# Attention and two expert layers in one Trainium2 kernel: the routing of the last batch issued in groups, and the weight pieces of the first slots split by one engine

## The chip, the core and the metric

The kernel runs on one core of a Trainium2 chip. The core has a matrix engine (TensorE, PE in the rows, with its weight loads as PEld), a vector engine (VectorE, DVE), a scalar engine (ScalarE, ACT), a general engine (GpSimd, POOL) and a sync engine (SyncE, SP) that here only issues transfers. Each engine works through its own list of instructions in the order in which the kernel was written, and waits at an instruction until what it needs is there. The metric is the device time of one execution in microseconds; lower is better.

## The reference, cut to what matters

```python
# attention, 4 batches x 12 heads x 448 rows x 64, scores capped with tanh
scores = cap * np.tanh(scale * np.matmul(q, k.T) / cap)
...
# a dense layer, 1792 rows x 768, hidden width 1536
(silu(x @ w_gate) * (x @ w_val)) @ w_out
# a routed layer, 8 experts, 768 -> 1024 -> 768
do_compute = x @ w_skip > 0
e_idx = np.argmax(x @ w_route, axis=1)
gate_w = softmax(x @ w_route)[arange, e_idx]
for e in range(8):
    h = np.maximum(x[e_idx == e] @ w1[e], 0.0)
    y[e_idx == e] = gate_w * (h @ w2[e])
out[do_compute] = x + y
```

## The kernel before, in words

**Batches.** Attention and the dense layer run batch by batch. The dense layer of a batch is 36 *units* of 18 matmuls each, so 144 units in all (`W_END`); a unit w multiplies with weights that ACT rounds (`wh`) and DVE turns into a remainder (`wl`), because every product is made of three: high times high, high times low, low times high.

**Slots.** The routed layer works in *slots*: 128 rows that go to one expert. Slot 0 and the expert of slot 1 (`FETCHED = 2`) are chosen while batch 3 is still in the dense layer, from batches 0 to 2 alone. The rest (which rows go to slots 1 to 7, and the experts of slots 2 to 7) is known only when the last batch has been routed. A slot takes eight *pieces* of expert weights, 128 x 1536 numbers each. Four go into `first(0)` to `first(3)`, nine matmuls each into `ph`, then a relu into `hid` and a transpose through `tp` into `rh` and `rl` (high and low part of the hidden rows); four go into `second(0)` to `second(3)`, twelve matmuls each into `py`. `finish` multiplies with the gate, adds the rows (`o`) and scatters them to the output.

**A piece's way.** SP loads it into a raw buffer (`load_next`), ACT copies its high part (`gh`, line 915), an engine subtracts for the low part (`gl`, line 356), PE uses both, and the pair of buffers serves again. `split_next` does the two steps in the middle. From slot 1 on (`so["auto"]`) each call of `piece()` first splits ahead until as many pieces are ready as there are pairs.

**Between the dense layer and slot 1.** What each engine does from unit 144 on is written out by hand in the table `LATE`: `first` and `second` are PE's work for slot 0, `splitV` and `splitP` split a piece on DVE or on POOL, and each `route` is one step of `last_routed`, the routing of the last batch. That is a chain of some 40 small DVE instructions: `choose` (which expert), a product on PE (`count_up`, into `last`), `ranks`, `last_tiles`, `places`, `last_at`, `entries`, a second product on PE (`listed`, line 257), which gives the row numbers (`idx`) for the gathers, then `experts` (`es`, which SP waits for before it can load slot 2) and at the end `gates`, whose list needs a third product. `turn_h` makes `rh` on ACT and `rl` on DVE; `turn_x(1)` transposes the gathered rows of slot 1.

**Rooms.** Before, 14 raw buffers and 4 pairs; a pair is taken in a fixed rotation.

Of the kernel before, what the change touches and what calls it, by code (L numbers as in the profile page):

```python
# [26 lines left out]

LENGTHS = (5, 6, 5, 6, 5, 5)

NOW = 7  # L30


STEPS = {0: 6, 1: 2, 2: 3, 3: 3, 4: 3, 5: 4, None: 4}
# [24 lines left out]
    chain store  # L58
""".split()
LATE = """  # L60
    route route route route route route route route route route splitV first1 route route route route route
    route route route splitP route route route route route hidden0 first2 route route route splitP route route
    route route first3 route splitV hidden1 second0 route route route splitP route splitP route second1 second2
    route route route route route route route route route route route splitV route rows1 gather gather second3
    route route splitV gather gather gather gather
""".split()


# [1 line left out]
def tile_attn_moe_moe(  # L70
# [311 lines left out]
    def whole(exact):  # L382
        with ExitStack() as ph:
# [449 lines left out]
            def open_early():  # L833
                right.close()
                _, pool = pools("right")
                p = pool("early", 1)
                psum = pool("ps_e", 1, space=PSUM)
                so["raw"] += [x[:, 0:PIECE] for x in pair_room + [head_room]]
                so["raw"] += [p.tile([128, PIECE], F32, name="raw3")]
                so["pair"] += [[p.tile([128, PIECE], F32R, name=f"{n}{i}") for n in ("gh", "gl")] for i in range(3)]  # L840
                so["xg"].append(p.tile([128, DM], F32, name="xg0"))
                so["x"] = [p.tile([128, KD, 128], F32R, name=n) for n in ("xgh", "xgl")]
                so["h"] = [[p.tile([128, KF2 // 2, 128], F32R, name=f"{n}{i}") for n in ("rh", "rl")] for i in range(2)]
                so["room"] = p.tile([128, 1024], F32, name="big_room")[0:T]
                so["row"] = p.tile([128, S], F32, name="row2")
                so["ph"] = [psum.tile([128, 512], F32, name=f"ph{i}") for i in range(2)]
                so["tp"] = [psum.tile([128, 512], F32, name=f"tp{i}") for i in range(2)]
                nc.gpsimd.memset(so["xg"][0], 0.0)

            def open_late():  # L850
                left.close()
                _, pool = pools("left")
                p = pool("late", 1)
                psum = pool("ps_l", 1, space=PSUM)
                so["xg"] += [p.tile([128, DM], F32, name=f"xg{i}") for i in range(1, NSTATIC)]
                raws_ = [p.tile([128, PIECE], F32, name=f"raw{i}") for i in range(7, 14)]
                so["raw"] += raws_[:NOW]
                so["spare"] = raws_[NOW:]
                so["pair"] += [[p.tile([128, PIECE], F32R, name=f"{n}3") for n in ("gh", "gl")]]
                so["late"] = p.tile([T, 1600], F32, name="late_room")  # L860
                so["hid"] = p.tile([128, F2], F32, name="hid")
                so["o"] = [p.tile([128, DM], F32, name=f"o{i}") for i in range(3)]
                so["last"] = psum.tile([128, 512], F32, name="last")
                so["py"] = psum.tile([128, 2, 512], F32, name="py")
                for xg in so["xg"][1:]:
                    nc.gpsimd.memset(xg, 0.0)
# [9 lines left out]
                    bounds_check=end - 1, oob_is_err=False,  # L876
                )

            def turned(high, low, src):
# [7 lines left out]
                split_low(nc.vector, low, tp, high)  # L887
# [6 lines left out]
            def turn_h(half):  # L894
                rh, rl = so["h"][half]
                turned(rh, rl, so["hid"][:, 512 * half:512 * half + 512])


            coming, todo, held, ready, made = [], [], [], [], [0]

            def load_next():
                while so["raw"] and not todo:
# [6 lines left out]
                load_piece(held[-1], todo.pop(0))  # L909
                return True  # L910

            def split_next(engine):
                raw = held.pop(0)
                wh, wl = so["pair"][made[0] % len(so["pair"])]
                nc.scalar.copy(wh, raw)  # L915
                split_low(engine, wl, raw, wh)
                so["raw"].append(raw)
                made[0] += 1
                ready.append((wh, wl))

            def begin_loads():
                coming.extend(range(FETCHED))
# [3 lines left out]
            def piece():  # L926
                while load_next():
                    pass
                while so["auto"] and held and len(ready) < len(so["pair"]):
                    split_next(nc.vector)  # L930
                return ready.pop(0)

            def mm3_(ps, sh, sl, wh, wl, start, stop):
# [4 lines left out]
            def first(i):  # L938

                xh, xl = so["x"]  # L940
                half, k0 = i // 2, 3 * (i % 2)
                wh, wl = piece()
                for kk in range(3):
                    c = slice(512 * kk, 512 * kk + 512)
                    mm3_(so["ph"][half], xh[:, k0 + kk], xl[:, k0 + kk], wh[:, c], wl[:, c],
                         k0 + kk == 0, k0 + kk == KD - 1)
                if i % 2:
                    nc.scalar.activation(
                        out=so["hid"][:, 512 * half:512 * half + 512], in_=so["ph"][half], func=ACTF.Relu
                    )  # L950

            def second(i):

                rh, rl = so["h"][i // 2]
                wh, wl = piece()
                HD = DM // 2
                for f in range(2):
                    f2 = 2 * (i % 2) + f
                    for half in range(2):
                        c = slice(DM * f + HD * half, DM * f + HD * half + HD)  # L960
                        mm3_(so["py"][:, half, 0:HD], rh[:, f2], rl[:, f2], wh[:, c], wl[:, c],
                             i == 0 and f == 0, i == 3 and f == 1)

            def finish(s):
                HD = DM // 2
# [185 lines left out]
            for w in range(W_END):  # L1151
# [22 lines left out]
            open_late()  # L1174


            def last_routed():
                b = B - 1
                last, take = so["last"], scratch(so["late"])
                yield from choose(b, take)  # L1180
                yield count_up(b, last)
                yield from ranks(b, take)
                yield from last_tiles(take)
                yield from places(b, take)
                yield from last_at(b, take)
                rt.pop("ah", None)
                yield from entries(b, rt["at"], (tok,), take)
                yield listed(last[:, 0:MAXSLOT])
                V.tensor_tensor(idx, lists[:, 0], last[:, 0:MAXSLOT], op=ALU.add)
                yield next_gathered()  # L1190
                so["raw"] += so["spare"]
                while load_next():
                    pass
                yield from experts(take)
                coming.extend(range(FETCHED, NSTATIC))
                yield from gates(b)
                yield from entries(b, rt["at"], (gate,), take)
                yield listed(last[:, 64:64 + MAXSLOT])
                yield V.tensor_tensor(lists[:, 1], lists[:, 1], last[:, 64:64 + MAXSLOT], op=ALU.add)

            gathered = iter(range(1, NSTATIC))

            def next_gathered():
# [1 line left out]
                    gather(s)  # L1205
                    return

            routing = last_routed()
            so["auto"] = False
            late = {  # L1210
                "route": lambda: next(routing, None), "splitV": lambda: split_next(V),
                "splitP": lambda: split_next(nc.gpsimd), "first1": lambda: first(1), "first2": lambda: first(2),
                "first3": lambda: first(3), "hidden0": lambda: turn_h(0), "hidden1": lambda: turn_h(1),
                "second0": lambda: second(0), "second1": lambda: second(1), "second2": lambda: second(2),
                "second3": lambda: second(3), "rows1": lambda: turn_x(1), "gather": next_gathered,
            }
            for name in LATE:
                late[name]()
            any(False for _ in routing)
            any(gather(s) for s in gathered)  # L1220
            so["auto"] = True
            finish(0)
# [104 lines left out]
```

## Time and profile before

| | us |
|---|---|
| median of 3 runs | 933.44 |
| lowest and highest | 932.9, 936.52 |
| the profiled execution, device time | 933.06 |
| its span in the profile | 930.8 |
| PE busy | 897.0 (96%) |
| DVE busy | 635.2 (68%) |
| ACT busy | 509.0 (55%) |
| POOL busy | 124.3 (13%) |

The span is the time from the first to the last instruction of the profiled execution; 2.3 us of its device time lie around it. The shares are averages over stages of different kinds.

### The profile page before, as it was taken

The numbers are of one execution on the slowest core, as the hardware profiler recorded it, in microseconds if no ns is written. First come the engines' busy times: TensorE is split into PE (matmuls) and PEld (weight loads), VectorE is DVE, ScalarE is ACT, GpSimd is POOL, SyncE is SP. The second block draws the span as 40 slices with busy tenths as digits, with TensorE's granted clock in tenths as the row PEclk, the third lists the DMA queues.
The fourth block names the chain that finished last, engine by engine and source line by source line (L and its number), as shares of the span: only waits on it lengthen the run. The fifth ranks groups of instructions, "written<-read, shape, count | busy, mean of one in ns | idle before, by whom it ended". The sixth has DMA issues, their size and how long they took to land.

```text
span 930.8 us, 12697 instructions
## 1 busy us (share of the span) xinstructions
PE 897.0 (96%) x4708; PEld 700.5 (75%) x4708; DVE 635.2 (68%) x916; ACT 509.0 (55%) x587; POOL 124.3 (13%) x76
## 2 busy tenths in 40 slices
PE   5999999999899999999999999999999995999996
PEld 2336776677567877777777877889999885988996
DVE  1868999897736755736566664446755458899994
ACT  5996675666355455545554546233333432778883
POOL 1000000000002221122302223000000036311001
PEclk9999999999899999999999999999999997899999
DMA  6996888888668234432744222453364373999940
GB/s 125 212 239 180 232 247 245 234 230 242 155 128 199 79 93 128 98 93 62 180 120 127 88 93 68 97 129 137 118 226 165 81 217 126 378 392 397 395 178 7
DMA packets 226336, 161.50 MB, mean 174 GB/s; under 512 B 159180, under 2 KB 186828, under 8 KB 226256
## 3 DMA queue, kind: packets, MB, share of 16 engines
q1 hardware_dynamic: 224048, 157.12, 58.8%
q0 software_dynamic: 1280, 3.16, 0.9%
q8 instruction: 41, 0.67, 0.3%
q14 instruction: 39, 0.32, 0.1%
q10 hardware_dynamic: 928, 0.23, 0.1%
HBM read 140.80 MB, written 22.81 MB: 176 GB/s over the span
## 4 chain that ended last, share of the span: by engine, by line
PE 89%; DVE 3%; ACT 3%; SPq 2%; issue 1%; DMA 1%; POOL 0%; POOLq 0%; DVEq 0%
PE mo L681 20%; PE mo L682 19%; PE mo L683 19%; PE ps L459 7%; PE bank L514 6%; PE py L936 2%; PE py L934 2%; PE py L935 2%; PE ph L934 2%; PE ph L935 2%; PE ph L936 2%; PE mo L548 1%; SPq L370 1%; PE tp L885 1%; PE mo L751 1%
## 5 line engine op out<-in xcount | busy, mean ns | idle before, releaser
L681 PE MATMUL mo<-xhl,wh 128*128 128x448 f32 x576 | 215.0, 373 | 0.0
L683 PE MATMUL mo<-xhl,wl 128*128 128x448 f32 x576 | 210.4, 365 | 0.0
L682 PE MATMUL mo<-xhl,wh 128*128 128x448 f32 x576 | 210.3, 365 | 0.0
L356 DVE TENSOR_TENSOR wl<-raw,wh 128x768 fp32r<-128x768 f32 x108 | 115.3, 1068 | 76.4 <-ACT wh L668 75.0
L668 ACT CAST wh<-raw 128x768 fp32r<-128x768 f32 x108 | 89.7, 831 | 87.5 <-PE mo L682 62.6
L681 PEld LDWEIGHTS mo<-xhl,wh 128*128 128x128 f32 x576 | 108.1, 188 | 27.3 <-issue 8.1
L683 PEld LDWEIGHTS mo<-xhl,wl 128*128 128x128 f32 x576 | 108.2, 188 | 8.9 <-DVE wl L356 0.2
L682 PEld LDWEIGHTS mo<-xhl,wh 128*128 128x128 f32 x576 | 108.3, 188 | 7.9
L681 PE MATMUL mo<-hh,wh 128*128 128x448 f32 x288 | 108.4, 376 | 1.0 <-ACT x L728 1.0
L682 PE MATMUL mo<-hl,wh 128*128 128x448 f32 x288 | 105.5, 366 | 0.0
L683 PE MATMUL mo<-hh,wl 128*128 128x448 f32 x288 | 105.4, 366 | 0.0
L720 ACT ACTIVATE s<-mo 128x448 f32<-128x448 f32 x48 | 26.0, 541 | 114.3 <-PE mo L683 111.4
L459 PE MATMUL ps<-qkt 64*112 64x448 f32 x368 | 82.6, 568 | 0.0
L503 POOL TENSOR_TENSOR sums<-arena 112x896 f32<-112x896 f32 x11 | 23.2, 2113 | 393.4 <-ACT arena L475 393.4
L468 ACT ACTIVATE arena<-ps,inv_sb 112x896 f32<-112x896 f32 x72 | 68.7, 1006 | 5.4 <-PE ps L459 5.3
L475 ACT ACTIVATE arena<-arena,cap_sb 112x1792 f32<-112x1792 f32 x36 | 64.5, 1793 | 1.1
L681 PEld LDWEIGHTS mo<-hh,wh 128*128 128x128 f32 x288 | 54.3, 188 | 14.0 <-issue 7.9
L356 DVE TENSOR_TENSOR gl<-raw,gh 128x1536 fp32r<-128x1536 f32 x33 | 57.7, 1757 | 6.4 <-ACT gh L915 5.8
L723 DVE SCALAR_TENSOR_TENSOR s<-s,mo 128x448 f32<-128x448 f32 x48 | 29.6, 617 | 42.8 <-PE mo L683 42.5
L683 PEld LDWEIGHTS mo<-hh,wl 128*128 128x128 f32 x288 | 54.2, 188 | 4.6
L682 PEld LDWEIGHTS mo<-hl,wh 128*128 128x128 f32 x288 | 54.3, 188 | 4.0
L514 PE MATMUL bank<-arena,arena 112*64 112x448 f32 x264 | 54.9, 548 | 1.7 <-ACT arena L475 0.8
(241 smaller groups left out, 1434.3 us busy)
## 6 DMA issues: line engine op xcount, KB each, us to landing
raw<-ws SPq DMA_DIRECT2D x54, 768.0 KB, 4.6
raw<-in_moe_w_dram SPq DMA_DIRECT2D x33, 768.0 KB, 12.5
ws<-w SPq DMA_DIRECT2D x36, 384.0 KB, 5.8
more<-in_moe_w_dram SPq DMA_DIRECT2D x15, 768.0 KB, 13.2
raw<-in_moe_w_gate_dram SPq DMA_DIRECT2D x12, 768.0 KB, 5.6
raw<-in_moe_w_val_dram SPq DMA_DIRECT2D x12, 768.0 KB, 5.7
raw<-in_moe_w_out_dram SPq DMA_DIRECT2D x12, 768.0 KB, 5.3
pair_room<-in_moe_w_dram SPq DMA_DIRECT2D x11, 768.0 KB, 12.9
```

The source lines that it names most:

```text
L356: engine.tensor_tensor(low, full, high.bitcast(F32), op=ALU.subtract)
L459: nc.tensor.matmul(ps[:, i, 0:S], lhsT=qkt[rows_, 1, T * c:T * c + T], rhs=qkt[rows_, 0], start=True, stop=True)
L468: nc.scalar.activation(out=t[:, j], in_=ps[:, :, 0:S], func=ACTF.Tanh, scale=inv_sb[0:T])
L475: nc.scalar.activation(out=ts[part], in_=ts[part], func=ACTF.Exp, scale=cap_sb[0:T])
L514: nc.tensor.matmul(pv[64 * i:64 * i + 64], lhsT=hd["vn"][:, i, c], rhs=hd["t"][c // 2][:, c % 2, i], start=c == 0, stop=c == NC - 1,)
L668: nc.scalar.copy(wh, w32s[w])
L681: nc.tensor.matmul(ps, lhsT=wh, rhs=mh, start=start, stop=False)
L682: nc.tensor.matmul(ps, lhsT=wh, rhs=ml, start=False, stop=False)
L683: nc.tensor.matmul(ps, lhsT=wl, rhs=mh, start=False, stop=stop)
L934: nc.tensor.matmul(ps, lhsT=sh, rhs=wh, start=start, stop=False)
L935: nc.tensor.matmul(ps, lhsT=sh, rhs=wl, start=False, stop=False)
L936: nc.tensor.matmul(ps, lhsT=sl, rhs=wh, start=False, stop=stop)
```

## The change

The table `LATE` is written anew. Each group of routing steps is issued whole (`choose`, `ranks`, `gates`, ...), not step by step, and `gates` stands ahead of `ranks`. There is no `splitP`: all pieces are split on DVE. Five pieces, not three, are split before the dense layer ends, after units 133, 134, 135, 137 and 138 (`SPLITS`), not after 139, 140 and 141. `listed` is called once with both lists side by side. `turn_h` can leave its low part for later (`lows0`, `lows1`). The room `more` becomes two pairs, so there are 6 pairs and 10 raw buffers; a pair is now free again when PE's matmuls with it have been written (a queue, not a rotation), and at most four pieces are split ahead (`AHEAD`).

```diff
+AHEAD = 4
+SPLITS = (11, 10, 9, 7, 6)
...
 LATE = """
-    route route route route route route route route route route splitV first1 route route route route route
-    route route route splitP route route route route route hidden0 first2 route route route splitP route route
-    route route first3 route splitV hidden1 second0 route route route splitP route splitP route second1 second2
-    route route route route route route route route route route route splitV route rows1 gather gather second3
-    route route splitV gather gather gather gather
+    choose first1 count first2 hidden0 gates ranks tiles places lows0 at entries first3 split second0 listed hidden1
+    gather experts lows1 second1 split second2 split rows1 second3 gather gather gather gather gather gather
 """.split()
...
-                raws_ = [p.tile([128, PIECE], F32, name=f"raw{i}") for i in range(7, 14)]
-                so["raw"] += raws_[:NOW]
-                so["spare"] = raws_[NOW:]
-                so["pair"] += [[p.tile([128, PIECE], F32R, name=f"{n}3") for n in ("gh", "gl")]]
+                so["raw"] += [p.tile([128, PIECE], F32, name=f"raw{i}") for i in range(7)]
+                so["pair"] += [[p.tile([128, PIECE], F32R, name=f"{n}4") for n in ("gh", "gl")]]
...
-            def split_next(engine):
-                raw = held.pop(0)
-                wh, wl = so["pair"][made[0] % len(so["pair"])]
+            def split_next():
+                raw, parts = held.pop(0), so["pair"].pop(0)
+                wh, wl = parts
                 nc.scalar.copy(wh, raw)
-                split_low(engine, wl, raw, wh)
+                split_low(nc.vector, wl, raw, wh)
                 so["raw"].append(raw)
...
-                while so["auto"] and held and len(ready) < len(so["pair"]):
-                    split_next(nc.vector)
+                while so["auto"] and held and so["pair"] and len(ready) < AHEAD:
+                    split_next()
...
-                    more = keep_p.tile([128, 2 * KD * S], F32, tag="xhl", name="more")
-                    so["raw"] += [more[:, PIECE * i:PIECE * i + PIECE] for i in range(3)]
+                    more = keep_p.tile([128, 2 * KD * S], F32R, tag="xhl", name="more")
+                    so["pair"] += [[more[:, 0:PIECE], more[:, PIECE:2 * PIECE]], [more[:, 2 * PIECE:3 * PIECE], so["odd"]]]
...
-                if w >= W_END - 5 and len(ready) < 3:
-                    split_next(V)
+                if W_END - w in SPLITS:
+                    split_next()
                     load_next()
...
+            def all_listed():
+                listed(last[:, 0:2 * MAXSLOT])
+                V.tensor_tensor(
+                    lists, lists, last[:, 0:2 * MAXSLOT].rearrange("p (a s) -> p a s", a=2), op=ALU.add
+                )
+                V.tensor_copy(idx, lists[:, 0])
...
             late = {
...
+                "split": split_next, "first1": lambda: first(1), "first2": lambda: first(2),
+                "first3": lambda: first(3), "hidden0": lambda: turn_h(0, 0), "hidden1": lambda: turn_h(1, 1),
+                "lows0": lambda: split_low(V, *lows.pop(0)), "lows1": lambda: split_low(V, *lows.pop(1)),
```

The lists of the engines show it at three places. The first is DVE just after the last batch's experts have been chosen. `above` is the last step of `choose`, `gl` the low part of a piece; before:

```order
L189 TENSOR_TENSOR above<-above,oh 112x8 x4
L356 TENSOR_TENSOR gl_15746<-raw_14522,gh_15745 128x1536
L190 TENSOR_TENSOR late_room<-lg,late_room 112x32
L202 TENSOR_TENSOR late_room<-last,count 112x32
L203 TENSOR_TENSOR late_room<-late_room,oh 112x32
```

And after the change, where the three `gate` rows are the steps of `gates`:

```order
L188 TENSOR_TENSOR above<-above,oh 112x8 x4
L189 TENSOR_TENSOR late_room<-lg,late_room 112x32
L212 TENSOR_REDUCE gate<-late_room 112x4
L213 TENSOR_SCALAR gate<-gate 112x4
L214 RECIPROCAL gate<-gate 112x4
L201 TENSOR_TENSOR late_room<-last,count 112x32
L202 TENSOR_TENSOR late_room<-late_room,oh 112x32
```

The subtraction for a piece has left this place, and the gates, which stood at the end of the routing, now stand ahead of `ranks` (its first row is `late_room<-last,count`).

The second is ACT at the same time, from slot 0's first relu on. The exponential that the gates need is the one row on `late_room`; before:

```order
L948 ACTIVATE hid<-ph_14538 128x512
L915 CAST gh_14523<-more 128x1536
L886 CAST rh_14532<-tp_14541 128x512
L915 CAST gh_14525<-more 128x1536
L948 ACTIVATE hid<-ph_14539 128x512
L915 CAST gh_14527<-more 128x1536
L886 CAST rh_14534<-tp_14540 128x512
L915 CAST gh_15745<-pair_room_93 128x1536
L915 CAST gh_14523<-pair_room_94 128x1536
L212 ACTIVATE late_room<-late_room 112x32
```

And after:

```order
L950 ACTIVATE hid<-ph_14534 128x512
L885 CAST rh_14528<-tp_14537 128x512
L211 ACTIVATE late_room<-late_room 112x32
L950 ACTIVATE hid<-ph_14535 128x512
L917 CAST gh_14518<-head_room 128x1536
L885 CAST rh_14530<-tp_14536 128x512
L917 CAST gh_15733<-pair_room_93 128x1536
L917 CAST gh_14520<-pair_room_94 128x1536
```

Five of the casts have gone, and the exponential moved up, to right behind the evacuation of slot 0's first transpose (`rh`).

The third is DVE at the end of slot 0: `xgl` is the low part of slot 1's rows, `o` the end of slot 0. Before:

```order
L1199 TENSOR_TENSOR lists<-lists,last 128x21
L356 TENSOR_TENSOR gl_14526<-head_room,gh_14525 128x1536
L356 TENSOR_TENSOR xgl<-tp_14541,xgh 128x384
L356 TENSOR_TENSOR xgl<-tp_14540,xgh 128x384
L356 TENSOR_TENSOR gl_14528<-raw_15738,gh_14527 128x1536
L966 SCALAR_TENSOR_TENSOR o_15749<-py,lists,xg_14529 128x768
L356 TENSOR_TENSOR gl_15746<-raw_15739,gh_15745 128x1536
```

And after:

```order
L324 CAST es_i<-es 1x22
L355 TENSOR_TENSOR rl_14531<-tp_14536,rh_14530 128x512
L355 TENSOR_TENSOR gl_15734<-pair_room_93,gh_15733 128x1536
L355 TENSOR_TENSOR gl_14521<-pair_room_94,gh_14520 128x1536
L355 TENSOR_TENSOR xgl<-tp_14537,xgh 128x384
L355 TENSOR_TENSOR xgl<-tp_14536,xgh 128x384
L969 SCALAR_TENSOR_TENSOR o_15737<-py,lists,xg_14525 128x768
L355 TENSOR_TENSOR gl_14523<-raw_15726,gh_14522 128x1536
L355 TENSOR_TENSOR more<-raw_15727,more 128x1536
L355 TENSOR_TENSOR gl_14524<-raw_15728,more 128x1536
L355 TENSOR_TENSOR gl_14519<-raw_15729,gh_14518 128x1536
```

Before, three pieces of slot 1 are split ahead of `o` (one of them on POOL); after, the two `gl` rows ahead of `o` are slot 0's own last pieces, and slot 1's first four all stand behind `o`.

## Rows read from the trace of the kernel before

**Rows 1.** By stretch: length, busy PE, PEld, DVE, ACT, POOL; clock, DMA share, GB/s.

```profile
740.00:757.00 17.00, 17.00 (x96) 14.95 (x95) 9.39 (x10) 6.16 (x7) 0.00 (x0) 1.00 0.70 181
760.00:790.00 30.00, 20.01 (x92) 17.39 (x92) 27.42 (x53) 10.72 (x11) 18.12 (x10) 0.83 0.47 164
```

**Rows 2.** PE in order of time: start, duration, instruction, wait ahead of it.

```profile
245.36 0.40 PE L579 MATMUL bank<-dn,alike 64*64 64x14 f32 x4 [4.18 <-DVE dn L573]
...
763.81 0.66 PE L885 MATMUL tp<-ident,hid 128*128 128x128 f32 x4
...
774.68 0.69 PE L936 MATMUL py<-gh,rl 128*128 128x384 f32 x1 [4.35 <-DVE rl L356]
...
790.02 1.90 PE L257 MATMUL last<-late_room 112*128 112x21 f32 x8 [4.38 <-DVE late_room L252]
```

**Rows 3.** DVE in order of time: start, duration, instruction.

```profile
648.94 0.25 DVE L220 TENSOR_TENSOR big_room<-count,steps 112x112 f32<-112x112 f32 x1
...
765.31 3.46 DVE L203 TENSOR_TENSOR late_room<-late_room,oh 112x32 f32<-112x32 f32 x1
...
768.90 3.35 DVE L220 TENSOR_TENSOR late_room<-count,steps 112x112 f32<-112x112 f32 x1
...
781.10 7.66 DVE L322 TENSOR_TENSOR es<-es,early 112x21 f32<-112x21 f32 x1
```

**Rows 4.** POOL in order of time.

```profile
781.84 6.88 POOL L356 TENSOR_TENSOR gl<-pair_room,gh 128x1536 fp32r<-128x1536 f32 x2
...
794.98 0.99 POOL L873 DMA_INDIRECT xg<-out_dram,idx  x1 [0.30 <-issue]
```

**Rows 5.** The chain that ended last: start, duration, what.

```profile
709.90 0.82 PE bank L257 x8
...
775.69 0.32 PE py L935
...
810.14 0.17 PE py L936
...
815.17 0.23 PE ph L934
...
833.33 0.23 PE ph L934
```

**Rows 6.** DVE in order of time, further instructions.

```profile
772.28 0.27 DVE L221 TENSOR_REDUCE late_room<-late_room 112x8 f32<-112x112 f32 x1
...
773.94 0.69 DVE L356 TENSOR_TENSOR rl<-tp,rh 128x512 fp32r<-128x512 f32 x1
...
776.59 0.25 DVE L252 TENSOR_TENSOR late_room<-late_room,tok 112x84 f32<-112x84 f32 x1
...
779.91 0.16 DVE L318 TENSOR_TENSOR late_room<-late_room 112x8 f32<-112x8 f32 x1
...
795.19 1.76 DVE L356 TENSOR_TENSOR gl<-raw,gh 128x1536 fp32r<-128x1536 f32 x1 [0.46 <-ACT gh L915]
797.06 1.02 DVE L966 SCALAR_TENSOR_TENSOR o<-py,lists,xg 128x768 f32<-128x768 f32 x1
```

**Rows 7.** ACT in order of time.

```profile
765.02 0.59 ACT L886 CAST rh<-tp 128x512 fp32r<-128x512 f32 x1
...
779.71 0.23 ACT L212 ACTIVATE late_room<-late_room 112x32 f32<-112x32 f32 x1
```

**Rows 8.** Busy time by half microsecond, columns as in rows 1.

```profile
772.50:773.00 0.50, 0.00 (x0) 0.00 (x0) 0.43 (x3) 0.00 (x0) 0.00 (x0) 0.89 1.05 412
783.00:783.50 0.50, 0.50 (x4) 0.50 (x3) 0.50 (x1) 0.00 (x0) 0.50 (x1) 0.87 0.00 0
243.50:244.00 0.50, 0.00 (x0) 0.00 (x0) 0.50 (x2) 0.50 (x2) 0.00 (x0) 0.83 1.00 362
789.50:790.00 0.50, 0.00 (x0) 0.00 (x0) 0.42 (x2) 0.00 (x0) 0.40 (x1) 0.96 0.00 0
```

**Rows 9.** Transfers into `xg` (gathers), issue to landing.

```profile
DMA to landing us min/median/max: 2.7/7.1/7.5
```

More of the change, by code (lines that the diff above doesn't have):

```diff
@@ L28 @@
 LENGTHS = (5, 6, 5, 6, 5, 5)
-NOW = 7
+AHEAD = 4
+SPLITS = (11, 10, 9, 7, 6)
 STEPS = {0: 6, 1: 2, 2: 3, 3: 3, 4: 3, 5: 4, None: 4}
@@ L838, in open_early @@
                 so["raw"] += [x[:, 0:PIECE] for x in pair_room + [head_room]]
-                so["raw"] += [p.tile([128, PIECE], F32, name="raw3")]
                 so["pair"] += [[p.tile([128, PIECE], F32R, name=f"{n}{i}") for n in ("gh", "gl")] for i in range(3)]
+                so["odd"] = p.tile([128, PIECE], F32R, name="gl3")
                 so["xg"].append(p.tile([128, DM], F32, name="xg0"))
@@ L877, in gather, with turned @@
                 )
-            def turned(high, low, src):
+            lows = {}
+            def turned(high, low, src, later=None):
                 n = high.shape[1]
@@ L886, in turned @@
                 nc.scalar.copy(high, tp)
-                split_low(nc.vector, low, tp, high)
+                if later is None:
+                    split_low(nc.vector, low, tp, high)
+                else:
+                    lows[later] = low, tp, high
             def turn_x(s):
@@ L892, in turn_x, with turn_h @@
                     turned(xh[:, kk:kk + 3], xl[:, kk:kk + 3], so["xg"][s % NSTATIC][:, 128 * kk:128 * kk + 384])
-            def turn_h(half):
+            def turn_h(half, later=None):
                 rh, rl = so["h"][half]
-                turned(rh, rl, so["hid"][:, 512 * half:512 * half + 512])
-            coming, todo, held, ready, made = [], [], [], [], [0]
+                turned(rh, rl, so["hid"][:, 512 * half:512 * half + 512], later)
+            coming, todo, held, ready = [], [], [], []
             def load_next():
@@ L910, in load_next @@
                 return True
-            def split_next(engine):
-                raw = held.pop(0)
-                wh, wl = so["pair"][made[0] % len(so["pair"])]
+            def split_next():
+                raw, parts = held.pop(0), so["pair"].pop(0)
+                wh, wl = parts
                 nc.scalar.copy(wh, raw)
-                split_low(engine, wl, raw, wh)
+                split_low(nc.vector, wl, raw, wh)
                 so["raw"].append(raw)
-                made[0] += 1
-                ready.append((wh, wl))
+                ready.append(parts)
             def begin_loads():
@@ L941, in first @@
                 half, k0 = i // 2, 3 * (i % 2)
-                wh, wl = piece()
+                wh, wl = parts = piece()
                 for kk in range(3):
@@ L946, in first @@
                          k0 + kk == 0, k0 + kk == KD - 1)
+                so["pair"].append(parts)
                 if i % 2:
@@ L954, in second @@
                 rh, rl = so["h"][i // 2]
-                wh, wl = piece()
+                wh, wl = parts = piece()
                 HD = DM // 2
@@ L962, in second @@
                              i == 0 and f == 0, i == 3 and f == 1)
+                so["pair"].append(parts)
             def finish(s):
@@ L1174, in whole, with all_of, entered, experts_known @@
             open_late()
[L1177 to L1185, printed above, removed]
-                rt.pop("ah", None)
[L1187 to L1191, printed above, removed]
+            b, last, take = B - 1, so["last"], scratch(so["late"])
+            def all_of(*chains):
+                return lambda: [any(False for _ in chain()) for chain in chains]
+            def entered():
+                rt.pop("ah", None)
+                yield from entries(b, rt["at"], (tok, gate), take)
+            def all_listed():
[4 more added lines that the diff above has]
+                V.tensor_copy(idx, lists[:, 0])
+            def experts_known():
+                yield from experts(take)
+                coming.extend(range(FETCHED, NSTATIC))
                 while load_next():
                     pass
[L1194 to L1199, printed above, removed]
             gathered = iter(range(1, NSTATIC))
@@ L1206, in next_gathered @@
                     return
-            routing = last_routed()
             so["auto"] = False
+            while load_next():
+                pass
             late = {
-                "route": lambda: next(routing, None), "splitV": lambda: split_next(V),
-                "splitP": lambda: split_next(nc.gpsimd), "first1": lambda: first(1), "first2": lambda: first(2),
-                "first3": lambda: first(3), "hidden0": lambda: turn_h(0), "hidden1": lambda: turn_h(1),
+                "choose": all_of(lambda: choose(b, take)), "count": lambda: count_up(b, last),
+                "ranks": all_of(lambda: ranks(b, take)), "tiles": all_of(lambda: last_tiles(take)),
+                "places": all_of(lambda: places(b, take)), "at": all_of(lambda: last_at(b, take)),
+                "entries": all_of(entered), "listed": all_listed, "experts": all_of(experts_known),
+                "gates": all_of(lambda: gates(b)),
+                "split": split_next, "first1": lambda: first(1), "first2": lambda: first(2),
+                "first3": lambda: first(3), "hidden0": lambda: turn_h(0, 0), "hidden1": lambda: turn_h(1, 1),
+                "lows0": lambda: split_low(V, *lows.pop(0)), "lows1": lambda: split_low(V, *lows.pop(1)),
                 "second0": lambda: second(0), "second1": lambda: second(1), "second2": lambda: second(2),
@@ L1218, in whole @@
                 late[name]()
-            any(False for _ in routing)
             any(gather(s) for s in gathered)
```

## The prediction

> **What bounds the kernel now.** The first view is the busy time by stretch [rows 1]. Until 757 us PE is busy in every microsecond (17.00 of 17), with DVE at 9.39 and ACT at 6.16: nothing can be gained there, and there is room on both. Between 760 and 790 us PE is busy for 20.01 of 30 us, at a mean clock of 0.83. That is the stretch the change rewrites, and the only one that can become shorter. PE's own rows say where it stands [rows 2]: 4.35 us before 774.68, for the low part of slot 0's hidden rows, and 4.38 us before 790.02, for the gate list. Both come from DVE, so DVE is read next [rows 3]: three tiny instructions last 3.46, 3.35 and 7.66 us there, though the middle one took 0.25 us in the batch before (648.94). POOL's rows say what held them [rows 4]: its two splits from 781.84 run 6.88 us, to 788.72, and DVE's 7.66 us end at 788.76; another such pair lies beside the other two. Last comes the chain [rows 5]. It shows the price of a stall beyond its length: a 128 x 384 matmul goes by every 0.17 us at the full clock and every 0.32 us behind the first stall. And it shows that slots start 18.16 us apart from 815.17, slot 2's first matmul. From there both kernels do the same work, so I work out when that matmul starts after the change.
>
> **What costs nothing.** Two more early splits and a shift of three put 2 x 1.76 us [rows 6] more on DVE before 757, into a stretch with 7.6 us free under a busy PE; without that cover it would be 3.5 us. SP's loads wait for these splits, with two reads of dense weights and the row stores behind them; the units that need those reads come several units later, so I price it at nothing, at most one split (1.76 us). Fewer raw buffers (10 for 14): a piece is wanted every 18.16 / 8 = 2.27 us, so a buffer has over 20 us to be refilled. One set of products for two takes one of the two from PE.
>
> **The new walk through slot 0, at the full clock.** Without the splits on POOL the three held instructions fall back to some 0.2 us each. But the order makes a new wait. DVE now stands at the gates' first step, ahead of `ranks`, and that needs the exponential on ACT. On ACT the exponential is behind the copy of `rh`, which needs PE's transposes, and these now come behind `first(2)`. So: PE is through the routing's first product at 763.81 [rows 2], where the transposes used to start; nine matmuls at 0.23 us and four transposes (0.44 us) take it to 766.3, the results are there at 766.5, the copy takes 0.59 and the exponential 0.23 [rows 7]: 767.25. DVE, done with `choose` at 763.6, idles 3.65 us.
>
> From 767.25 the gates take three steps (0.5 us), `ranks` and the comparison 0.85 us (0.25 us for the comparison, 0.1 to 0.2 us for each of the other four). That is 768.6, where before the next step stood at 772.28. From there to the last `entries` step DVE took 776.59 + 0.25 - 772.28 = 4.56 us with one low part (0.69 us) inside [rows 6], and does the same now plus one more list (0.25 us): the low part of `rh` is ready at 771.7, the lists' input at 773.4.
>
> PE meanwhile ends `first(3)` at 768.4 and does two matmuls of `second(0)`; it stands from 768.9 to 771.7. **Stall 1** is 2.8 us, in place of 4.35. Ten matmuls lead to 773.45, the product of both lists (0.82 us, as in the earlier batches [rows 5]) to 774.3, the transposes to 774.75. Piece 5's split ends at 775.2, so `second(1)` runs to 777.1. On DVE follow the lists and the row numbers (0.35 us), then the experts: 1.2 us from the first step to the one that was held, as before (779.91 to 781.10), and 0.65 us for that one and its followers; I add 0.4 us for meeting gathers, between 0 and 1.0. That is 777.6. Then the second low part (0.69) and piece 6's split (1.76): 780.0. **Stall 2** is PE's 2.8 us from 777.2. `second(2)`, slot 1's transposes (0.66) and `second(3)` end at 784.7.
>
> Now the cost of having no piece ahead. Before, three pieces of slot 1 were split when slot 0 ended; now the first one's low part stands behind `o`, which needs the last matmul: 784.9 + 1.02 + 1.76 [rows 6] = 787.65. **Stall 3** holds PE, but for one matmul, from 784.7. From then DVE makes a piece every 1.7 us and PE eats one every 2.1, with one wait of 0.2 us for `rl`, and slot 1 ends at 805.7. From its second piece on the order again has four splits ahead, so I take the lag as paid once. At the full clock the sum is 815.17 - 805.7 = 9.5 us.
>
> **The clock.** The three stalls of over 4 us (two above, one of 4.18 us before 245.36 [rows 2]) all let the granted clock fall from full to half, 2.4 to 1.2 GHz [rows 8]: a mean of 0.89 over half a microsecond puts the fall at 772.9, 2.6 us after PE stopped; the others fell at 243.8 (2.65 us in) and at 789.96 (4.3 us in). It came back at 783.1, over 8 us after PE resumed. So a stall of 2.8 us is long enough by two cases of three and too short by the third. A fall in stall 1 slows ten matmuls (1.5 us), the product and the transposes; some of it is taken out of stall 2, and 1.5 us remain. A fall in stall 2 or 3 stays for 6 us or more of work at half speed, with little waiting left to absorb it: 2.5 to 3 us. I take stall 1 and one of the others: 1.5 + 2.5 = 4.0 us.
>
> The Trainium skill, page "TensorE: Matmul & The Clock Gate", section "HAM oscillation — how this bites in real kernels", warns only of gaps longer than these three. By it the clock would stay up and the sum would be the 9.5 us alone.
>
> **The sum** is 9.5 - 4.0 = 5.5 us, against the profiled execution: span 930.8 - 5.5 = 925.3, time 933.06 - 5.5 = 927.6. The median of the runs is 0.4 us above that execution; I leave the forecast where the sum puts it.
>
> **The rivals.**
> - *The clock holds in all three stalls.* 933.06 - 9.5 = 923.6. For it: each stall is shorter than the shortest with a fall. Against: two falls came 2.6 us in. 0.14. With one fall alone, 925 to 926.5: 0.2.
> - *The gathers take the place of POOL's splits.* All seven now follow each other on POOL while DVE works out the experts. If a gather held a DVE instruction as a split did, four small ones and two splits would wait up to 1.0 us each, 3 us in all: 930.5. Against: the gather at 794.98 [rows 4] lay beside a split that started at 795.19 and took its usual 1.76 us. To the same end leads a late gather: slot 1's transposes stand 5.8 us behind the issue, and landing took 2.7 to 7.5 us [rows 9], so up to 1.5 us; or a fall in all three stalls. Together 0.16. The Trainium skill, page "SBUF — State Buffer", section "SBUF: two separate sides", says that a GpSimd operation which reads this memory and a vector operation with two inputs in it exclude each other for a whole instruction. If a gather is such an operation, this rival is what it would do.
> - *Slower: the lag is paid in every slot.* If DVE cannot catch up, each later slot also waits about 2.5 us at its `o`, six more times: 923.6 + 15 = 938.6. It decides at a DVE load of 18.16 us per slot. Against: eight splits, two low parts (0.69), `xgl` (some 1.0) and `o` make 8 x 1.76 + 1.4 + 1.0 + 1.0 = 17.5 us. 0.05.
> - *The change does nothing here*, because DVE stands on the exponential as long as it was held before: 933. Only if stall 1 were 4.4 us again; with the walk above it is not. 0.03.
>
> **How the numbers follow.** My forecast, 927.6, has 0.42, and a range of its own of 926.6 to 928.6. The cases on both sides give 923.4 to 930.5 for 8 in 10. A change under 0.5% cannot be told from none here; 0.5% faster ends at 928.4. Most of the forecast's case and the two above it lie below: 0.68 faster; the rest of it, the gathers and no effect: 0.24; slower 0.08.
>
> **What would show it.** Right: DVE idle for over 3 us before the gates' first step, released by ACT; a PE wait of 2.5 to 3 us in `second(0)` on `rl`, one in `second(2)` on a piece's `gl`, one in slot 1's `first(0)`; no DVE instruction over 2 us; PE's clock at half somewhere between 770 and 797; slots 18.16 us apart from slot 2 on. Wrong: waits in later slots, small DVE rows stretched beside gathers, a gap ahead of slot 1's transposes, or stalls that fall together into one over 4 us.

## The result, and the profile after

The changed kernel takes 925.73 us (median of 6 runs, 924.29 to 926.08), the kernel before 932.62 us in the same set; the ratio is 0.9917, with a 95% interval from 0.9899 to 0.9935. The profiled execution took 925.63 us with a span of 923.8, 7.0 us under the span before. PE was busy for 893.8 us of it (97%), POOL for 109.3 (12%).

The view by stretch, columns as in [rows 1], with three half microseconds at the edges of the only stretch at half clock in these slots:

```profile
740.00:757.00 17.00, 17.00 (x97) 14.93 (x96) 7.08 (x11) 4.58 (x6) 0.00 (x0) 1.00 0.43 88
760.00:790.00 30.00, 24.20 (x120) 20.87 (x119) 20.05 (x60) 12.46 (x14) 11.51 (x13) 0.89 0.86 299
774.00:774.50 0.50, 0.50 (x5) 0.50 (x4) 0.47 (x4) 0.00 (x0) 0.00 (x0) 0.78 1.01 393
774.50:775.00 0.50, 0.50 (x3) 0.50 (x2) 0.50 (x2) 0.00 (x0) 0.00 (x0) 0.50 1.02 393
781.00:781.50 0.50, 0.50 (x3) 0.28 (x2) 0.50 (x2) 0.11 (x1) 0.50 (x1) 0.89 0.65 128
```

PE is busy for 24.20 us between 760 and 790, where it was busy for 20.01 [rows 1]. The clock is at half, 1.2 GHz, from 774.3 to 781.1 (a mean of 0.78 puts the fall 0.28 us into its half microsecond, one of 0.89 the rise 0.11 us into its own): 6.8 us, where before it was at half twice, from 772.9 to 783.1 and again from 789.96 [rows 8].

PE in order of time, the answer to [rows 2]:

```profile
246.38 0.39 PE L578 MATMUL bank<-dn,alike 64*64 64x14 f32 x4 [5.28 <-DVE dn L572]
...
758.83 0.50 PE L935 MATMUL ph<-gh,xgh 128*128 128x512 f32 x1
...
772.86 0.44 PE L937 MATMUL py<-more,rl 128*128 128x384 f32 x1 [2.82 <-DVE rl L355]
...
775.08 1.77 PE L256 MATMUL last<-late_room 112*128 112x42 f32 x8
...
777.86 0.52 PE L936 MATMUL py<-gl,rh 128*128 128x384 f32 x1
...
786.43 0.49 PE L935 MATMUL ph<-gh,xgh 128*128 128x512 f32 x1
789.33 0.50 PE L936 MATMUL ph<-gl,xgh 128*128 128x512 f32 x1 [2.40 <-DVE gl L355]
...
807.57 0.39 PE L935 MATMUL ph<-more,xgh 128*128 128x512 f32 x1
```

Two waits are left, 2.82 us in `second(0)` and 2.40 in slot 1's `first(0)`, in place of 4.35 and 4.38. The matmul at 777.86 runs in the slow stretch (0.52 us for 0.34). Slot 0's first product starts at 758.83 and slot 2's at 807.57: 48.74 us. In the kernel before the same view has them at 757.64 and 815.01: 57.37 us. I use this distance for all runs below, since it leaves out what happens before slot 0.

DVE, the answer to [rows 3, 6], and POOL, the answer to [rows 4]:

```profile
768.39 0.19 DVE L212 TENSOR_REDUCE gate<-late_room 112x4 f32<-112x32 f32 x1 [3.71 <-ACT late_room L211]
...
769.10 0.19 DVE L202 TENSOR_TENSOR late_room<-late_room,oh 112x32 f32<-112x32 f32 x1
...
769.43 0.27 DVE L219 TENSOR_TENSOR late_room<-count,steps 112x112 f32<-112x112 f32 x1
...
778.29 0.15 DVE L320 TENSOR_REDUCE late_room<-late_room 112x1 f32<-112x8 f32 x1
778.41 0.18 DVE L321 TENSOR_TENSOR es<-es,early 112x21 f32<-112x21 f32 x1
...
779.77 3.43 DVE L355 TENSOR_TENSOR gl<-pair_room,gh 128x1536 fp32r<-128x1536 f32 x2 [0.17 <-issue]
...
787.52 1.75 DVE L355 TENSOR_TENSOR gl<-raw,gh 128x1536 fp32r<-128x1536 f32 x1
```

```profile
778.10 1.01 POOL L870 DMA_INDIRECT xg<-out_dram,idx  x1 [14.64 <-DVE late_room L231]
...
780.72 1.68 POOL L870 DMA_INDIRECT xg<-out_dram,idx  x1 [0.30 <-issue]
```

The three held instructions (now L202, L219 and L321) take 0.19, 0.27 and 0.18 us for 3.46, 3.35 and 7.66. In their place DVE stands 3.71 us for the exponential. The last of the three lies beside a gather (778.10 to 779.11) and is not longer for it.

The chain, the answer to [rows 5]:

```profile
775.28 1.57 PE last L256 x8
...
807.73 0.23 PE ph L935
...
825.99 0.24 PE ph L935
```

Slot 2 starts 7.44 us earlier than before, and the slots follow each other at 18.26 us, not 18.16.

### The profile page after: what moved, and what is told of

The parts are those of the page before. It is cut to its first block, busy times and chain, and to the rows that moved or that the text cites. A ratio compares the mean times of both kernels' runs of the same rounds, so it can differ in the third digit from the quotient of the medians.

```text
span 923.8 us, 12689 instructions
## 1 busy us (share of the span) xinstructions
PE 893.8 (97%) x4700; PEld 696.2 (75%) x4700; DVE 628.3 (68%) x920; ACT 506.7 (55%) x587; POOL 109.3 (12%) x72
## 4 chain that ended last, share of the span: by engine, by line
PE 86%; DVE 5%; ACT 4%; DMA 2%; issue 2%; SPq 1%; POOL 0%; POOLq 0%; DVEq 0%; ACTq 0%
PE mo L680 19%; PE mo L682 17%; PE mo L681 17%; PE ps L458 7%; PE bank L513 6%; PE py L937 3%; PE py L936 3%; PE py L935 2%; PE ph L936 2%; PE ph L935 2%; PE ph L937 2%; PE tp L884 1%; PE mo L547 1%; ACT arena L467 1%; ACT arena L474 1%
## 5 line engine op out<-in xcount | busy, mean ns | idle before, releaser
L458 PEld LDWEIGHTS ps<-qkt 64*112 64x112 f32 x368 | 29.6, 175 | 34.9 <-issue 29.3
```

The costliest lines, as they stand in the source:

```text
L458: nc.tensor.matmul(ps[:, i, 0:S], lhsT=qkt[rows_, 1, T * c:T * c + T], rhs=qkt[rows_, 0], start=True, stop=True)
```

## The experiments

All runs in one table: the waits of PE of 0.8 us and more in slots 0 and 1, the time at half clock between 757 and 810 us (from the edges in the view by stretch), and the distance from slot 0's first product to slot 2's. The runs were made in four sets. Each ratio is against the kernel before in the same set, whose median was 932.62, 933.20, 933.37 or 933.02 us, so compare ratios, not medians, across sets. The last three columns come from one profiled execution of each kernel.

| | median us | ratio (95%) | PE's waits, us | half clock, us | slot 0 to 2, us |
|---|---|---|---|---|---|
| before | 932.62 | 1 | 4.35, 4.38 | 10.2, 6.8 | 57.37 |
| the change | 925.73 | 0.9917 (0.9899 to 0.9935) | 2.82, 2.40 | 6.8 | 48.74 |
| changed_again | 924.50 | 0.9910 (0.9896 to 0.9924) | 2.81, 2.40 | 6.8 | 48.79 |
| before_vector_splits | 923.27 | 0.9892 (0.9876 to 0.9908) | 1.57, 2.66 | 3.4 | 47.44 |
| gates_behind_places | 924.36 | 0.9907 (0.9891 to 0.9922) | 1.90, 2.38 | 3.4, 3.4 | 48.01 |
| filled_stall | 925.74 | 0.9919 (0.9905 to 0.9934) | 1.90, 2.38 | 3.4, 3.4 | 50.78 |
| two_splits_ahead | 922.06 | 0.9883 (0.9866 to 0.9901) | 2.82 | 6.8 | 46.74 |
| three_early | 927.06 | 0.9925 (0.9910 to 0.9941) | 2.81, 2.39 | 6.8, 3.4 | 51.06 |
| combined | 918.74 | 0.9842 (0.9830 to 0.9855) | 0.99, 1.57 | none | 44.00 |
| combined_rows_later | 920.46 | 0.9866 (0.9852 to 0.9881) | 1.01, 0.84 | none | 44.30 |
| cast_ahead | 919.16 | 0.9856 (0.9837 to 0.9876) | 1.35, 1.20 | none | 43.64 |
| four_pairs_later | 919.67 | 0.9869 (0.9850 to 0.9888) | 1.01, 1.58 | none | 43.98 |

`changed_again` is the changed kernel run once more, as it is. Its two waits, its 6.8 us at half clock, the lack of a fall in slot 1 and the slots 18.23 to 18.28 us apart come back. The wait in batch 0's attention does not: 3.85 us, for 5.28.

In `gates_behind_places`, `filled_stall` and `three_early` the profiled execution was the slowest of the six (926.80, 927.79 and 928.04 us; the fastest took 922.70, 924.25 and 924.06). These are also the three kernels whose trace has a second fall of the clock, in slot 1. Whether their faster executions had that fall no trace shows, so their distances may lie at the slow end.

**The splits alone.** The kernel before, with its POOL splits on DVE:

```diff
-                "splitP": lambda: split_next(nc.gpsimd), "first1": lambda: first(1), "first2": lambda: first(2),
+                "splitP": lambda: split_next(V), "first1": lambda: first(1), "first2": lambda: first(2),
```

> The kernel before with its four POOL splits done by DVE, in the same places, and nothing else changed. Theory 1 (the three held DVE instructions were the cost; DVE does a split in 1.76 us, and 4 x 1.76 is less than the 13.9 us of held instructions): no DVE row over 2 us, the first wait on rl 1 to 2 us in place of 4.35, the second of 4.38 under 4, less time at half clock, slot 2 starts 8 to 10 us earlier: 923 to 926, as good as the whole change. Theory 2 (the grouping, the early splits and the single product bring a part of the gain, since four more splits lie between the routing steps on DVE): 928 to 931. Theory 3 (the splits on DVE cost the path as much as the holds did): 933.

Theory 1. No single DVE instruction there takes over 2 us. The three that were held, and PE's two waits, are

```profile
766.31 0.19 DVE L203 TENSOR_TENSOR late_room<-late_room,oh 112x32 f32<-112x32 f32 x1
766.64 0.27 DVE L220 TENSOR_TENSOR late_room<-count,steps 112x112 f32<-112x112 f32 x1
781.13 0.18 DVE L322 TENSOR_TENSOR es<-es,early 112x21 f32<-112x21 f32 x1
```

```profile
774.64 1.07 PE L257 MATMUL last<-late_room 112*128 112x21 f32 x8 [1.57 <-DVE late_room L252]
...
782.66 1.07 PE L257 MATMUL last<-late_room 112*128 112x21 f32 x8 [2.66 <-DVE late_room L252]
```

The first wait was expected on `rl`; it is on the entries behind it. From slot 0 to slot 2 this one edit is worth 57.37 - 47.44 = 9.9 us, more than the whole change (8.6), and the slots behind stay at 18.16 to 18.17 us. By these traces the gain is the move of the splits; the rest of the change costs 1.3 us in slots 0 and 1, and some 0.5 behind them. The ratios (0.9892 for 0.9917 and 0.9910) point the same way, but their intervals overlap.

**The wait for the exponential.** The changed kernel's table, with the gates further back:

```diff
-    choose first1 count first2 hidden0 gates ranks tiles places lows0 at entries first3 split second0 listed hidden1
+    choose first1 count first2 hidden0 ranks tiles places lows0 at gates entries first3 split second0 listed hidden1
```

> The changed kernel with the three gate steps moved on DVE from ahead of the ranks to behind the places, so that DVE no longer stands at the exponential. Theory 1 (the wait for the exponential is on the path): the 3.7 us of idle DVE ahead of the gates are gone, the low part of rh is ready about 768.9 instead of 772.8, the wait of 2.8 us in second(0) is under 0.3 us, PE's clock does not fall at 774; the wait then stands ahead of second(2) (2 to 3 us, for the piece split behind the experts), the 2.4 us in slot 1 stay: slot 1 starts some 4 us earlier, 921 to 922.5 in place of 925.7. Theory 2 (the wait only changes place: the gathers or the experts bind behind it): 925 to 926, with a wait ahead of slot 1's transposes or one of over 4 us in second(2).

The mechanism is theory 1's, the time nearly theory 2's. The wait in `second(0)` is gone, and the clock stays up until 780. Slot 0 takes 25.4 us from its first product to slot 1's, for 27.6. Then a fall came behind each of the two waits that were left:

```profile
779.62 0.44 PE L936 MATMUL py<-gl,rh 128*128 128x384 f32 x1 [1.90 <-DVE gl L355]
...
788.91 0.50 PE L936 MATMUL ph<-gl,xgh 128*128 128x512 f32 x1 [2.38 <-DVE gl L355]
```

```profile
780.00:780.50 0.50, 0.50 (x4) 0.50 (x3) 0.50 (x1) 0.00 (x0) 0.50 (x1) 0.50 1.03 399
790.50:791.00 0.50, 0.50 (x3) 0.34 (x2) 0.50 (x2) 0.50 (x1) 0.00 (x0) 0.50 0.59 176
```

Slot 1 takes 22.6 us for 21.1, as the second fall halves the clock for 3.4 us behind the wait of 2.38 us; behind the 2.40 us of the changed kernel there was none. In this execution 0.7 of the 2.2 us won in slot 0 remain.

**The clock by itself.** Products that keep PE busy while it would wait for `rl`:

```diff
+            def fill():
+                for _ in range(16):
+                    nc.tensor.matmul(so["py"][:, 0, 0:384], lhsT=so["h"][0][0][:, 0], rhs=ready[0][0][:, 0:384],
+                                     start=True, stop=True)
...
-first3 split second0 listed hidden1
+first3 split fill second0 listed hidden1
```

> The changed kernel with 16 extra 128 x 384 products on PE ahead of second(0), into a tile that second(0) then overwrites; they take 16 x 0.17 = 2.8 us, as long as PE stands there for rl. Theory 1 (the fall of the clock at 774 comes from this standstill and costs little, since the slow stretch takes the place of a wait of 2.8 us for piece 6): no fall between 770 and 785, and a wait of 2 to 2.8 us ahead of second(2) appears; 924.4 to 925.4 in place of 925.7. Theory 2 (the half clock costs what it takes from PE, 3.4 us in 6.9 us): 922 to 923. Theory 3 (the fall has to do with something else): the clock falls at 774 all the same, 925.7.

```profile
769.74 2.98 PE L1211 MATMUL py<-more,rh 128*128 128x384 f32 x16
...
780.78 0.65 PE L936 MATMUL py<-gl,rh 128*128 128x384 f32 x1 [1.90 <-DVE gl L355]
...
790.07 0.50 PE L936 MATMUL ph<-gl,xgh 128*128 128x512 f32 x1 [2.38 <-DVE gl L355]
```

The fall at 774 is gone, so it does come from that standstill, and the wait in `second(2)` that the prediction had, and the changed kernel did not show, is there: 1.90 us. But a fall came behind each of the two waits, and the distance is 2.0 us longer than with the wait left empty, in an execution some 2 us over the kernel's median. Theory 1 had the mechanism, but not the time. The median, 925.74, is that of theory 3, whose mechanism the trace refutes: a coincidence. A fall that was avoided in one place was met in the next.

**Two pieces ahead of `o`.**

```diff
-    gather experts lows1 second1 split second2 split rows1 second3 gather gather gather gather gather gather
+    gather experts lows1 second1 split second2 split split rows1 second3 split gather gather gather gather gather gather
```

> The changed kernel with two pieces of slot 1 split before slot 0's o, one behind second(2)'s splits and one behind second(3). Theory 1 (the wait of 2.4 us in slot 1's first product is the split that stands behind o, and it is paid once): that wait is gone, nothing comes in its place, 923.3 in place of 925.7, later slots as far apart as they were (18.26 us). Theory 2 (DVE is short of time in every slot, and two splits ahead only move the wait to the next slots): the wait turns up in slot 1's hidden rows or in slot 2, 925 to 926.

Theory 1, but for 0.63 us on `rl` in slot 1's `second(0)`: 46.74 us, 2.00 less (the expectation of the combined run, below, has 46.4 for it). The median is 3.7 us lower, more than these two slots account for. The later slots stay at 18.23 to 18.27. The lag is paid once.

**Three pieces early, as before.**

```diff
-SPLITS = (11, 10, 9, 7, 6)
+SPLITS = (11, 10, 9)
...
-    choose first1 count
+    choose split split first1 count
```

> The changed kernel with three pieces split before slot 0 in place of five; the two others are split on DVE behind choose, ahead of the gates. Theory 1 (DVE idles there 3.7 us for the exponential, and two splits take 2 x 1.75 us): no difference that can be told, 925.2 to 926.2, the gates' first step at the same distance from slot 0's first product, 9.6 us. Theory 2 (the early splits are a part of the gain): the gates start 3.5 us later, the first wait on rl grows to some 6 us, 928 to 930.

DVE did as theory 1 says: its two splits fill the wait, and the gates start 9.56 us behind slot 0's first product, in both kernels to the hundredth. The median, 927.06, lies between the two theories.

```profile
764.46 1.75 DVE L355 TENSOR_TENSOR more<-pair_room,more 128x1536 fp32r<-128x1536 f32 x1
766.13 1.75 DVE L355 TENSOR_TENSOR gl<-pair_room,more 128x1536 fp32r<-128x1536 f32 x1
768.24 0.19 DVE L212 TENSOR_REDUCE gate<-late_room 112x4 f32<-112x32 f32 x1 [0.36 <-ACT late_room L211]
```

The distance is 2.3 us longer all the same: 0.85 in slot 0 and 1.5 in slot 1, where a fall came behind the wait of 2.39 us. Of the 0.85, 0.28 stand already at the lists' product (16.53 us behind slot 0's first product, for 16.25): the clock fell 1.07 us behind the wait for `rl`, not 1.42, so more of `second(0)` ran at half clock. A wait of 0.27 us for a piece and one of 0.36 for the gather follow. So in this order the early splits bought nothing on the way to the gates.

**All three repairs.** The gates behind the places, two pieces ahead of `o`, the experts behind the last two splits:

```diff
+    choose first1 count first2 hidden0 ranks tiles places lows0 at gates entries first3 split second0 listed hidden1
+    gather lows1 second1 split second2 split experts split rows1 second3 split gather gather gather gather gather gather
```

> The changed kernel with the gates behind the places, two pieces of slot 1 split ahead of o, and the experts behind slot 0's last two splits on DVE. From first product of slot 0 to first product of slot 2 the changed kernel took 48.7 us, and 46.4 with two splits ahead alone. Theory 1 (DVE's order is all that PE waits for in these two slots): the waits on rl, in second(2) and in slot 1 are all under 1.2 us, no fall of the clock, 41 to 42 us, 917 to 919. Theory 2 (with slot 0 this early the first gather's landing binds, 4 us or more behind an issue that still has to follow the lists): PE or the cast of xg waits 1 to 3 us ahead of slot 1's transposes, 43 to 44.5 us, 919 to 920.5.

```profile
775.97 0.44 PE L936 MATMUL py<-gl,rh 128*128 128x384 f32 x1 [0.99 <-DVE gl L355]
779.74 0.88 PE L884 MATMUL tp<-ident,xg 128*128 128x128 f32 x6 [1.57 <-DMA xg<-out_dram,idx]
```

```profile
760.00:790.00 30.00, 26.59 (x145) 22.39 (x145) 25.54 (x63) 16.73 (x18) 12.25 (x11) 1.00 0.95 342
```

Theory 2 by its wait and by the distance, 44.00 us: PE now waits for the first gather. The clock holds throughout, which only theory 1 had said, and the median, 918.74, lies in theory 1's range. It is the fastest of all, 1.58% under the kernel before. The two repairs that were run alone gave 0.7 and 2.0 us of distance; with the third, which has no run of its own, they give 4.7.

**Around the gather.** Two ways to shorten that wait, and one run on the slots behind; each starts from the combined order.

```diff
-split experts split rows1 second3 split gather
+split experts split second3 rows1 split gather
```

> The combined order with slot 1's transposes behind second(3) in place of ahead of it, so that the gather has 2.1 us more. If the gather's landing binds in the combined order, the wait ahead of the transposes is gone or 2 us shorter, and a wait of about 1 us for the cast ahead of slot 1's first product stands in its place: 0.5 to 1.5 us faster than the combined order. If the gather does not bind, the cast's wait is all that is added: 0.5 to 1 us slower than it.

The wait for the gather is gone, but the transposes, the cast and the low parts of `xg` now stand between the slots: slot 1 has waits of 0.24, 0.84 and 0.23 us, the distance is 0.3 us longer and the median 1.7 us higher. The gather did bind, but the expected gain did not come.

```diff
-at gates entries first3 split second0 listed
+at gates entries cast first3 low second0 listed
```

(`cast` and `low` are the two halves of `split_next`: the copy on ACT and the subtraction on DVE.)

> The combined order with piece 5's cast on ACT ahead of the second half's relu, its low part where it was. In the combined order DVE stood 0.63 us for that cast, and lists, gather and slot 1's transposes are behind it. Theory 1 (the gather's landing binds slot 0's end): all of these are 0.6 us earlier, the wait of 0.28 us in second(1) is gone, the wait for the gather, 1.57 us, is about 0.6 us shorter; from slot 0's first product to slot 2's 43.4 us in place of 44.0, 918.2 in place of 918.7. Theory 2 (the landing depends on what else the DMA queues carry, not on the issue): that wait grows by as much as PE is earlier, 44.0 us, 918.7.

The gather is issued 15.09 us behind slot 0's first product, for 15.78, and its wait is 1.20 us, for 1.57. The wait of 0.28 us in `second(1)` is gone, but the one in `second(2)` grew from 0.99 to 1.35. The distance is 0.36 us shorter: between the theories, nearer the first. The medians, 919.16 and 918.74, do not tell the two kernels apart.

```diff
-                so["pair"].append(parts)
+                if not (so["auto"] and any(parts is k for k in so["kept"])):
+                    so["pair"].append(parts)
```

(`kept` holds the two pairs that lie in the old `xhl` rooms.)

> The combined order with the two pairs in the old xhl rooms used in slot 0 and once after it, and then no more: four pairs remain, as many as in the kernel before. Theory 1 (the slots are 0.09 us longer in the changed kernel, 18.25 for 18.16, because some weight pieces are read from these rooms): from slot 3 on they are 18.16 to 18.17 us apart, some 0.4 us less at the end, 918.3 in place of 918.7. Theory 2 (the rooms make no difference): 18.25. Theory 3 (four pairs are too few with this order): waits in the slots, over 18.3.

From slot 2 on the slots are 18.19 to 18.20 us apart, all alike, where the combined order has 18.26, 18.22, 18.28 in turn. No wait appears in the slots, against theory 3. So leaving these two pairs out makes 0.06 of the 0.09 us. The run has both fewer pairs and other rooms, so it does not show which of the two did it; what the other 0.03 is stays open. In the median it is not seen.

## Why the prediction was right, and where its sum was off

The forecast was 927.6 us, the measured median is 925.73. That is 0.9 us below the forecast's own range (926.6 to 928.6) and inside the wider one. Against the span of the profiled execution the forecast was -5.5 us, and -7.0 came (the device time moved by 7.4). To compare the walk, 1.19 us are taken off the times after, since slot 0's first product started that much later (758.83 for 757.64).

| step | predicted, us | after, less 1.19 |
|---|---|---|
| the exponential ends | 767.25 | 767.2 |
| DVE idle ahead of the gates | 3.65 | 3.71 |
| low part of `rh` ready | 771.7 | 771.6 |
| wait in `second(0)` | 2.8 | 2.82 |
| experts known | 777.6 | 777.9 |
| wait in `second(2)` | 2.8 | none |
| slot 0's last matmul ends | 784.7 | 785.2 |
| slot 1's first low part there | 787.65 | 788.1 |
| slot 2 starts (by the chain) | 805.7 at full clock, 809.7 with the falls | 806.5 |

- **The holds and the new wait** were right: the three instructions fell back to 0.2 us, and the exponential took their place, to within 0.1 us. (Of ACT's five casts in the stretch listed ahead of the prediction, three are left; what makes the wait is that none stands ahead of the exponential any more, only the copy of `rh`.)
- **The cost of no piece ahead** was right: 2.40 us and one matmul, paid once. Two splits moved ahead take it away.
- **The clock term was mis-sized.** The step was "I take stall 1 and one of the others: 1.5 + 2.5 = 4.0 us". At most 0.8 is left for it (806.5 - 805.7): 0.5 stood at slot 0's last matmul, and the other 0.3 came in slot 1, at the full clock. There was one fall, not two, which is the rival "with one fall alone, 925 to 926.5". And its cost lay where it was nearly free: it came 1.4 us after PE had resumed and slowed the lists' product (1.57 us in the chain for 0.82), the transposes and `second(1)`. PE lost half of 6.8 us, 3.4, just ahead of the place where the walk has it wait 2.8 us for piece 6; that wait vanished. With the fall taken away (the filled standstill) a wait is there, of 1.90 us.
- **Two small terms were missing.** The wait in batch 0's attention was 5.28 us for 4.18, in code that both kernels share: a 1.1 us later start, from one execution (3.85 in the changed kernel's second profile). And six slots of 18.25 us for 18.16 cost 0.5. The sum is then -9.5 + 0.8 + 1.2 + 0.5 = -7.0, as measured. So it is in part luck that the median came so near the forecast, and into the range of the one-fall rival: that rival has 1.4 to 2.9 us for the fall, and these two terms, which it does not have, made up for a cheaper fall.
- **Two sums are off** without moving the forecast by more than 0.2 us. The terms up to "experts known" add up to 777.8, not 777.6 (777.9 came), and a landing of 7.5 us against 5.8 is 1.7 us late at most, not 1.5.
- **The rivals.** The clock did not hold. No gather held a DVE instruction in these traces: the two splits beside them take 3.43 us, as ever, and it is the gather that is longer, 1.68 for 1.01. The lag is not paid in every slot. A late gather was no cost here, but it is what the combined order waits for.
- **What the prediction did not ask** is which part of the change carries the gain. By the traces, moving the splits does, alone. The rest put a wait of 3.7 us on DVE and one of 2.4 us on PE where there were none, and what early splits and grouping gave back was less. With the three repairs the same parts come to 918.74 us. What the grouping is worth by itself stays open: no run gives the kernel before, with its splits on DVE, the repairs without it.

The Trainium skill, page "SBUF — State Buffer", section "SBUF: two separate sides", states a rule that fits the holds: a GpSimd operation that reads this memory and a vector operation with two inputs in it exclude each other. The trace agrees for the splits (taking them off POOL ends the rows of 3.35 to 7.66 us); for the gathers no run shows a DVE row held. The Trainium skill, page "TensorE: Matmul & The Clock Gate", section "HAM oscillation — how this bites in real kernels", warns only of longer gaps; the traces show falls behind waits of 1.90 to 2.82 us, so here the measurement decides.

## What to carry to other kernels

When an engine's small instructions last for microseconds, move what holds them first, alone, and measure; a rewrite that comes with it can hide that it loses time. Where a group of steps is issued whole, look at what its first step waits for, and whether something behind it could run in the meantime; at a stage's end, let the next stage's first pieces stand ahead of the last result. A stall is to be weighed with the work behind it: a slow clock where the engine would have waited anyway cost little here (3.4 us of lost work, at most 0.8 us of time), and a stall that is removed may only hand its fall of the clock to the next.

## What the runs showed of the hardware

- The granted clock falls behind a wait, not only in it: with waits of 1.90 to 2.82 us it fell 0.1 to 2.1 us after PE had resumed, and stayed at half for 3.4 or 6.8 us. Waits of up to 1.58 us (eight in the four kernels of the combined order, one in the kernel with the splits alone) had no fall behind them. The same wait of 2.4 us in slot 1 had a fall of 3.4 us in three kernels, each profiled in the slowest of its executions, and none in the two profiles of the changed kernel. What decides it is not settled.
- A gather's instruction on POOL, 1.0 us by itself, took 3.09 us beside two DVE splits (`gates_behind_places`), which kept their 1.75 us each.
- Leaving out two pairs of buffers, in rooms of their own, made a slot 0.06 us of 18.25 shorter; whether by the rooms or by the number of pairs is open.
